# One-region weight layouts and two-tile normalisation at the start of an attention and gMLP block

## The chip, the cores and the metric

The kernel runs on one core of one Trainium2 chip. The core has a matrix engine (TensorE, PE in the profile), a vector engine (VectorE, DVE), a scalar engine (ScalarE, ACT), a general engine (GpSimd, POOL), a queue that issues transfers (SyncE, SP) and 16 DMA engines. Each engine takes its instructions in the order in which the program wrote them, and they meet only at semaphores. PE accumulates into 8 PSUM banks, which DVE and ACT read. The metric is the device time of one execution in microseconds, lower being better, as the median of several runs.

## The reference, cut to what matters

```python
mod = (silu(c) @ w_mod).reshape(1, 6, 1, 448)          # c: (1, 448), w_mod: (448, 2688)
sa, ca, ga, sb, cb, gb = mod[:, 0..5]
h = layernorm(x) * (1 + ca) + sa                        # x: (1, 2048, 448)
qkv = h @ wqkv                                          # wqkv: (448, 1344): q | k | v, 16 heads of 28
x = x + ga * (softmax(q @ k.T * 28**-0.5) @ v) @ wo
h = layernorm(x) * (1 + cb) + sb
z = gelu(h @ w_in); z1, z2 = halves of z (896 each); z2 = layernorm(z2)
x = x + gb * ((z1 * (w_sp @ z2 + b_sp)) @ w_out)        # w_sp: (2048, 2048)
```

All of it is in float32. The change touches only the first three lines and the product with `wqkv`. The other lines take most of the time.

## The kernel before, in words

The kernel keeps float32 accuracy by splitting operands into a high part, rounded for the fast matmul format, and a low part, the rest. A product then takes three matmuls per pair of blocks. Because 448 = 3 x 128 + 64, a product with a depth of 448 takes the eleven steps of the list `STEPS`. Each step `(a, b)` multiplies slot `a` of the one operand by slot `b` of the other. Slots 0, 1, 2 are high parts, 3, 4, 5 the low parts of the same blocks, 6 and 7 hold the last 64 rows, high and low. `STEPS_MAIN` needs slots 0 to 5, and `STEPS_Z` are the two steps on slot 6 of the first operand.

**The rows.** The 2048 rows of `x` are handled in four groups `g` of four tiles `t` of 128 rows. For each group: DVE takes mean and variance of each tile (`ln_stat`, two instructions a tile); POOL turns the variances into 1/sqrt (`ln_rs`, which calls `rstd_of`, two instructions, an addition and a power); DVE normalises (`ln_norm`, L257) and ACT copies 64 columns so that the last block is doubled (L265); PE transposes (L117, sixteen 128x128 pieces in four banks, `c` = 0 to 3); ACT applies scale and shift (L124) and rounds to the high part (L131); DVE subtracts to get the low part (`sub`, L84). The result is `hT[g]`, and its slots come in the order c = 0, 2, 1, 3. `ln_next(g)` does the last three steps for group `g` and, between them, the statistics of group `g + 1`; the power and the normalisation of group `g + 1` come after all four statistics.

**The weights.** `w_mod` is loaded in three pairs of 896 columns, each as four blocks `k` of 112 rows (`load_mod`, L168). The first pair gives `sa` and `ca`: `mod_acc` multiplies the blocks by silu(c) and adds them on DVE (L224, L226), `mod_last` adds the last block in small pieces (L355), PE sums over the partitions. Until `ca` and `sa` are there, no `hT` can be made. `wqkv` is loaded in three parts of columns, each in four row blocks: `v` (columns 896 to 1343), `a` (0 to 511) and `b` (512 to 895), by `load_w`. The last row block has 64 rows and is loaded twice (`load_z`, L87 and L88). Part `v` becomes `wv`; `qk_part` (in it `weight_part`, L95 on ACT for the high part and L84 on DVE for the low part) turns a row block `i` of `a` and `b` into `wqk`. The row blocks come in the order 0, 2, 1, 3.

**The order.** There is no planner here: each engine does what the text of the program lists, in that order. After the first group's `hT[0]` PE computes V of the first four tiles (`v_mm`, L273, 44 matmuls), then `qk_unit((0, 3), 0)`, two blocks of q and k at a time over the eleven steps (L288, 22 matmuls), then the transposes of group 1 (in `ln_next(1)`), the blocks 1 and 2 (22 matmuls, L288), the V of tiles 4 and 5 (22 matmuls, L273), the transposes of group 2, and so on. `qk_unit` ends with ACT writing the high part from PSUM (L298) and DVE the low part (L84, `ql`), after which the two banks are free, and SP stores both to scratch memory. Seven PSUM banks go round in one ring, in the order of `bank(...)` calls. Short matmuls on idle data (`pe_fill`, L215) fill gaps of PE in the first 18 us.

**SP** issues all these transfers in one queue, with eight semaphores in turn, so a transfer's issue waits until the eighth before it has landed, and for its buffer.

Later stages (the attention, the output projection, the gMLP) are not touched.

Of the kernel before, what the change touches and what calls it, by code (L numbers as in the profile page):

```python
# [8 lines left out]
F32 = mybir.dt.float32  # L9
# [7 lines left out]
S, D, H, DH, FH = 2048, 448, 16, 28, 896  # L17
# [11 lines left out]
STEPS = STEPS_MAIN + STEPS_Z  # L29
# [1 line left out]


@with_exitstack
def tile_adaln_mha_gmlp(ctx, tc, x, wqkv, wo, w_in, w_spT, b_sp, w_out, cT, w_mod, out):
# [48 lines left out]
    def sub(eng, dst, a, hi):  # L83
        eng.tensor_tensor(out=dst, in0=a, in1=hi.bitcast(F32), op=ALU.subtract)  # L84

    def load_z(eng, dst, src):
        eng.dma_start(dst[0:64], src)  # L87
        eng.dma_start(dst[64:128], src)  # L88

    def weight_part(dst, i, raw, hi_eng, lo_eng, zero=True, c0=0):  # L90

        cs = slice(c0, c0 + raw.shape[-1])
        h = dst[:, i if i < 3 else 6, cs]
        if hi_eng is act:
            act.activation(h, raw, AF.Copy)  # L95
        else:
            hi_eng.tensor_copy(h, raw)
        if i < 3:
            sub(lo_eng, dst[:, 3 + i, cs], raw, h)
        else:  # L100
            sub(lo_eng, dst[0:64, 7, cs], raw[0:64], h[0:64])
            if zero:
                pool.memset(dst[64:128, 7, cs].bitcast(F32), 0.0)

    def rstd_of(var, rs, n):

        pool.tensor_scalar(out=rs, in0=var, scalar1=EPS, scalar2=None, op0=ALU.add)
        pool.tensor_tensor(out=rs, in0=rs, in1=mhalf[:, :n], op=ALU.pow)

    def ln_transpose(xns, full_pool, dsts, scol, bcol, engs, los=(pool,) * 4, mid=None, after=None):  # L110

        tps = []
        for c in range(4):
            tp = bank("tp")
            tps.append(tp)
            for t in range(4):
                pe.transpose(tp[:, t * 128 : (t + 1) * 128], xns[t][:, c * 128 : (c + 1) * 128], ident)  # L117
        if mid:
            mid()
        for c in (0, 2, 1, 3):  # L120
            tp = tps[c]
            f = full_pool.tile([128, 512], F32, name="hfull")
            if engs[c] is act:
                act.activation(f, tp, AF.Identity, scale=scol[:, c : c + 1], bias=bcol[:, c : c + 1])  # L124
            else:
                engs[c].tensor_scalar(
                    out=f, in0=tp, scalar1=scol[:, c : c + 1], scalar2=bcol[:, c : c + 1], op0=ALU.mult, op1=ALU.add
                )
            hi = dsts[:, c if c < 3 else 6, :]
            if engs[c] is act:  # L130
                act.activation(hi, f, AF.Copy)  # L131
            else:
                engs[c].tensor_copy(hi, f)
            if c < 3:
                sub(los[c], dsts[:, 3 + c, :], f, hi)
            else:
                sub(los[c], hi[64:128], f[64:128], hi[64:128])
            if after:
                after(c)
# [16 lines left out]
    e1 = early.enter_context(tc.tile_pool(name="e1", bufs=2))  # L156
# [3 lines left out]
    wms, xts, raws = {}, {}, {}  # L160

    def bank(name):
        return ring.tile([128, 512], F32, name=name, tag="s")

    def load_mod(pair, eng):
        for k in range(4):
            wms[pair, k] = e1.tile([112, 2, D], F32, name="wm", tag=("wm", "wm", "raw")[pair], bufs=4)
            eng.dma_start(wms[pair, k], w_mod[:, pair, k])  # L168

    def load_x(g, eng):  # L170
        xg = e1.tile([128, 4, D], F32, name="xg")
# [3 lines left out]
            xts[4 * g + t] = xg[:, t, :]  # L175


    PARTS = {"v": (2 * D, D, "raw"), "a": (0, 512, "wm"), "b": (512, 384, "raw")}

    def load_w(kind, i, eng):  # L180
        c0, n, tag = PARTS[kind]
        raw = e1.tile([128, 2 * D], F32, name="raw", tag=tag, bufs=4)[:, :n]
        if i < 3:
            eng.dma_start(raw, wqkv[i * 128 : (i + 1) * 128, c0 : c0 + n])
        else:
            load_z(eng, raw, wqkv[384:448, c0 : c0 + n])
# [54 lines left out]
    def ln_stat(g, ts):  # L241
        if g not in mv1:
            mv1[g] = e1.tile([128, 4, 2], F32, name="mv"), e1.tile([128, 4], F32, name="rs")
        for t in ts:
            st = e1.tile([128, 6], F32, name="st", bufs=4)
            dve.bn_stats(out=st, in_=xts[4 * g + t])
            dve.bn_aggr(out=mv1[g][0][:, t, :], in_=st)

    def ln_rs(g, a, e):
        mv, rs = mv1[g]  # L250
        rstd_of(mv[:, a:e, 1], rs[:, a:e], e - a)

    def ln_norm(g, ts):
        mv, rs = mv1[g]
        for t in ts:
            xn = e1.tile([128, 512], F32, name="xn", bufs=4)
            dve.tensor_scalar(  # L257
                out=xn[:, :D],
                in0=xts.pop(4 * g + t),
                scalar1=mv[:, t, 0:1],  # L260
                scalar2=rs[:, t : t + 1],
                op0=ALU.subtract,
                op1=ALU.mult,
            )
            act.activation(xn[:, D:], xn[:, 384:D], AF.Copy)  # L265
            xn1.setdefault(g, []).append(xn)

    def v_mm(kts, steps=STEPS, own=None):
        pvs = [ps_o.tile([128, 512], F32, name="pv", tag="o") if kt == own else bank("pv") for kt in kts]
        for j, (a, b) in enumerate(steps):  # L270
            for kt, pv in zip(kts, pvs):
                g, t = divmod(kt, 4)
                pe.matmul(pv[:, :D], hT[g][:, a, t * 128 : (t + 1) * 128], wv[:, b, :], start=j == 0, stop=j == NST - 1)  # L273
        return list(zip(kts, pvs))

    def v_copy(kt, pv):
        act.activation(V[:, kt, :, 0:DH], pv[:, :D].rearrange("p (h d) -> p h d", d=DH), AF.Copy)
# [1 line left out]
    def v_tile(kt):  # L279
        v_copy(*v_mm((kt,))[0])  # L280

    def qk_unit(ms, g, mid=None):
        pqs = [bank("pq") for _ in ms]
        for j, (a, b) in enumerate(STEPS):
            if mid and j in mid:
                mid[j]()
            for m, pq in zip(ms, pqs):
                pe.matmul(pq, wqk[:, b, m * 128 : (m + 1) * 128], hT[g][:, a, :], start=j == 0, stop=j == NST - 1)  # L288
        for m, pq in zip(ms, pqs):
            hi = stage.tile([128, 512], F32R, name="qh")  # L290
            lo = stage2.tile([128, 512], F32R, name="ql")
            if mid:
                f = stage.tile([128, 512], F32, name="qf")
                act.activation(f, pq, AF.Copy)
                act.activation(hi, f, AF.Copy)
                sub(pool, lo, f, hi)
            else:
                act.activation(hi, pq, AF.Copy)  # L298
# [90 lines left out]
    for i in (0, 2, 1, 3):  # L389
        load_w("a", i, sp)  # L390
# [32 lines left out]
    for i in (0, 2, 1, 3):  # L423
        load_w("b", i, sp)
    pvs = v_mm((0, 1, 3, 2), [STEPS[j] for j in (0, 1, 2, 3, 6, 4, 5, 7, 8, 9, 10)], 3)
    ln_stat(1, (0, 1))
    qk_part("a", 0, dve)
    qk_part("a", 2, dve)
    ln_stat(1, (2, 3))
    ln_rs(1, 0, 4)  # L430
    qk_part("a", 1, dve)
    qk_part("a", 3, dve)
    load_mod(1, sp)
    for a in pvs:
        v_copy(*a)
    ln_norm(1, range(4))
    qk_unit((0, 3), 0)

    def ln_next(g):

        if g + 1 < NG:
            ln_transpose(
                xn1.pop(g), e1, hT[g], cols["ca"], cols["sa"], (act,) * 4, (dve,) * 4, None,
                lambda c: ln_stat(g + 1, ((0, 2, 1, 3).index(c),)),
            )
            ln_rs(g + 1, 0, 4)
            ln_norm(g + 1, range(4))
        else:
            ln_transpose(xn1.pop(g), e1, hT[g], cols["ca"], cols["sa"], (act,) * 4, (dve,) * 4)

    ln_next(1)
    load_x(3, sp)
    qk_unit((1,), 0)
    qk_unit((2,), 0)
    for i in (0, 2, 1, 3):
        qk_part("b", i, dve)
    load_mod(2, sp)
    for g in range(1, NG):
        if g == 3:
# [32 lines left out]
        if g + 1 < NG:  # L492
            ln_next(g + 1)
# [831 lines left out]
```

## Time and profile before

| | us |
|---|---|
| median of 3 runs | 1411.46 (1411.13 to 1413.48) |
| the profiled execution's own time | 1415.13 |
| its span, from the first to the last instruction | 1413.3 |
| PE busy | 1399.0 (99%) |
| DVE busy | 1011.3 (72%) |
| ACT busy | 787.5 (56%) |
| POOL busy | 284.9 (20%) |

Times are counted from the first instruction of the profiled execution. A row of the timeline gives start, time, engine, line, operation, the names written and read, the shapes and the count; in brackets stands how long the engine had been idle and what ended that. Rows that follow each other on one engine start a little before the row ahead of them has ended, since instructions are pipelined; a distance between two starts is what an instruction costs in a stream. A row of the chain gives start, length and what. A row of the waits gives who waited for whom, the total, the number of times and the longest. A row of the windows gives a stretch, its length, the busy time of each engine with the number of instructions in parentheses, the granted PE clock, the busy share of the 16 DMA engines and the GB/s that they moved.

### The profile page before, as it was taken

What the parts mean: (1) busy time and instruction counts of PE and PEld (TensorE: products, weight loads), DVE (VectorE), ACT (ScalarE), POOL (GpSimd) and SP (SyncE); (2) the same over time, 40 slices, a digit from 0 to 9 for tenths busy, and PEclk for the clock granted to TensorE, in tenths of its full rate; (3) what the DMA queues carried; (4) which work ended last, traced back from release to release, by engine and by line L of the source; (5) the groups of instructions that cost most, each with busy time, mean ns of one, the idle gap of its engine ahead of it and who ended that gap; (6) DMA issues with size and microseconds to landing.
All of it is one profiled execution on the core that took longest, in us unless ns stands there. A gap on an engine that the chain in (4) does not pass through costs nothing.

```text
span 1413.3 us, 20323 instructions
## 1 busy us (share of the span) xinstructions
PE 1399.0 (99%) x7180; PEld 985.4 (70%) x7180; DVE 1011.3 (72%) x1700; ACT 787.5 (56%) x1532; POOL 284.9 (20%) x276
## 2 busy tenths in 40 slices
PE   8999999999999999999999999999999999999998
PEld 7888655555555555555555555988998888887888
DVE  7778888888888888888888850751366655677474
ACT  3723677777777777777677779363243543434211
POOL 3033312212314243313200021000142430001000
PEclk9999999999999999999999999999999999999999
DMA  9564635555455556654423001434103333444453
GB/s 247 162 177 154 189 104 175 166 160 152 157 166 160 159 164 179 175 154 154 120 68 75 21 18 58 172 122 138 45 15 105 105 112 112 151 139 136 136 176 112
DMA packets 98252, 186.99 MB, mean 132 GB/s; under 512 B 16614, under 2 KB 28006, under 8 KB 95606
## 3 DMA queue, kind: packets, MB, share of 16 engines
q1 hardware_dynamic: 95722, 181.87, 42.5%
q10 hardware_dynamic: 2430, 3.84, 0.7%
q8 instruction: 56, 0.92, 0.3%
q14 instruction: 44, 0.36, 0.1%
HBM read 130.42 MB, written 50.45 MB: 128 GB/s over the span
## 4 chain that ended last, share of the span: by engine, by line
PE 95%; DVE 2%; DMA 2%; ACT 1%; issue 0%; POOL 0%; SPq 0%; ACTq 0%; DVEq 0%
PE st_ps L559 19%; PE o_ps L574 17%; PE mt L528 17%; PE acc L1099 6%; PE acc L1098 6%; PE acc L1100 6%; PE z_ps L1024 5%; PE z_ps L910 5%; PE pq L288 4%; PE wo_ps L780 3%; PE pv L273 2%; PE y_ps L1205 2%; PE y_ps L1206 2%; PE y_ps L1204 2%; DMA raw_sp<-ws_scr 1%; PE tp L117 1%
## 5 line engine op out<-in xcount | busy, mean ns | idle before, releaser
L533 DVE TENSOR_REDUCE pm<-mt 128x1 f32<-128x512 f32 x1024 | 631.6, 682 | 110.3 <-PE mt L528 110.2
L563 ACT ACTIVATE P<-st_ps 128x512 f32<-128x512 f32 x1024 | 513.2, 622 | 151.6 <-PE st_ps L559 151.2
L559 PE MATMUL st_ps<-qst,kst 128*128 128x512 f32 x1024 | 408.0, 409 | 0.1
L528 PE MATMUL mt<-kst,qst 128*128 128x512 f32 x1024 | 403.0, 394 | 0.0
L559 PEld LDWEIGHTS st_ps<-qst,kst 128*128 128x128 f32 x1024 | 191.0, 187 | 150.2 <-issue 82.2
L574 PE MATMUL o_ps<-P,V 128*32 128x512 f32 x2048 | 247.5, 598 | 0.0
L528 PEld LDWEIGHTS mt<-kst,qst 128*128 128x128 f32 x1024 | 192.5, 188 | 33.0 <-ACT P L563 0.7
L986 ACT ACTIVATE wsp_h<-raw_sp 128x512 fp32r<-128x512 f32 x112 | 70.1, 631 | 172.8 <-PE acc L1100 106.4
L681 POOL TENSOR_TENSOR ws_raw<-ws_raw 128x512 f32<-128x512 f32 x80 | 103.0, 1287 | 280.3 <-DMA ws_raw<-in_w_spT_dram 280.1
L84 DVE TENSOR_TENSOR wsp_l<-raw_sp,wsp_h 128x512 fp32r<-128x512 f32 x112 | 81.1, 735 | 90.7 <-ACT wsp_h L986 89.9
L574 PEld LDWEIGHTS o_ps<-P,V 128*32 128x32 f32 x2048 | 54.1, 109 | 123.9 <-issue 116.7
L1099 PE MATMUL acc<-wsp_l,heapA 128*128 128x512 f32 x224 | 88.2, 394 | 1.8 <-DVE wsp_l L84 1.8
L1098 PE MATMUL acc<-wsp_h,heapA 128*128 128x512 f32 x224 | 88.0, 393 | 1.2 <-ACT wsp_h L986 1.2
L1100 PE MATMUL acc<-wsp_h,heapA 128*128 128x512 f32 x224 | 87.9, 392 | 0.0
L1099 PE MATMUL acc<-wsp_l,heapB 128*128 128x512 f32 x174 | 67.7, 389 | 0.0
L1098 PE MATMUL acc<-wsp_h,heapB 128*128 128x512 f32 x174 | 67.7, 389 | 0.0
L1100 PE MATMUL acc<-wsp_h,heapB 128*128 128x512 f32 x174 | 67.7, 389 | 0.0
L288 PE MATMUL pq<-heapD,heapD 128*128 128x512 f32 x196 | 62.3, 392 | 0.0
L1028 DVE BATCH_NORM_STATS2 stz<-z 128x6 f32<-128x448 f32 x32 | 19.9, 625 | 50.4 <-ACT z L1027 30.1
L1099 PEld LDWEIGHTS acc<-wsp_l,heapA 128*128 128x128 f32 x224 | 42.3, 189 | 11.2 <-DVE wsp_l L84 2.5
L1098 PEld LDWEIGHTS acc<-wsp_h,heapA 128*128 128x128 f32 x224 | 42.5, 190 | 10.7 <-ACT wsp_h L986 1.6
L1100 PEld LDWEIGHTS acc<-wsp_h,heapA 128*128 128x128 f32 x224 | 42.5, 190 | 9.0
(205 smaller groups left out, 1594.8 us busy)
## 6 DMA issues: line engine op xcount, KB each, us to landing
ws_raw<-in_w_spT_dram SPq DMA_DIRECT2D x160, 256.0 KB
ws_scr<-ws_raw SPq DMA_DIRECT2D x80, 256.0 KB
raw_sp<-ws_scr SPq DMA_DIRECT2D x80, 256.0 KB
kst<-qk_scr SPq DMA_DIRECT2D x45, 224.0 KB
qst<-qk_scr SPq DMA_DIRECT2D x45, 224.0 KB
raw_sp<-in_w_spT_dram SPq DMA_DIRECT2D x32, 256.0 KB
qk_scr<-qh SPq DMA_DIRECT2D x28, 256.0 KB
qk_scr<-ql SPq DMA_DIRECT2D x28, 256.0 KB
```

Of the source, the lines that this page charges most:

```text
L84: eng.tensor_tensor(out=dst, in0=a, in1=hi.bitcast(F32), op=ALU.subtract)
L288: pe.matmul(pq, wqk[:, b, m * 128 : (m + 1) * 128], hT[g][:, a, :], start=j == 0, stop=j == NST - 1)
L528: pe.matmul(mt, qst[h % 3][:, t * 128 : (t + 1) * 128], kst[h % 3][:, kb * 512 : (kb + 1) * 512], start=True, stop=True)
L533: dve.tensor_reduce(out=pms[h][:, t, kb : kb + 1], in_=mt, axis=AX.X, op=ALU.max)
L559: pe.matmul(st, kst[h % 3][:, kt * 128 : (kt + 1) * 128], qst[h % 3][:, qb * 512 : (qb + 1) * 512], start=True, stop=True)
L563: act.activation(p, st, AF.Exp, scale=SCALE)
L574: pe.matmul(otile[h][32 * qb : 32 * qb + 32, :], V[:, kt, h, :], ptiles.pop((u, qb)), start=kt == 0, stop=kt == NT - 1)
L681: pool.tensor_tensor(out=a, in0=a, in1=b, op=SUMS[i // 16][2])
L910: pe.matmul(ps_t, w1[:, b, f * 128 : (f + 1) * 128], h2T[g][:, a, :], start=j == 0, stop=j == NST - 1)
L1098: pe.matmul(acc[i], zh, hi, start=st == 0, stop=False)
L1099: pe.matmul(acc[i], zh, lo, start=False, stop=False)
L1100: pe.matmul(acc[i], zl, hi, start=False, stop=st == 7)
```

## The change

Four things change.

1. On the host `w_mod` is stored with pair and block outermost, so that one transfer of 112 x 896 values reads 401,408 consecutive bytes (before, rows of 3,584 bytes 43,008 apart), and `wqkv` is stored as three arrays, `w_v`, `w_a`, `w_b`, so that a row block is consecutive too (before, rows of 1,792, 2,048 or 1,536 bytes 5,376 apart). The sizes and the number of the transfers and their order in the queue stay.
2. For group 1 the statistics of all four tiles come ahead of the first two `qk_part("a", ...)`, the powers are taken for two tiles at a time, and the normalisation of tiles 0 and 1 (with its ACT copies) stands between the second and the third `qk_part("a", ...)`; tiles 2 and 3 stay behind the copies of V.
3. In `ln_next` the power of two tiles follows the second and the fourth statistics, and tiles 0 and 1 are normalised behind the third (that is, ahead of c = 3); tiles 2 and 3 stay at the end.
4. `qk_unit((0, 3), 0)` takes its steps in the order `HI_FIRST`: first the seven with a high weight slot (0, 1, 2, 6), then the four with a low one (3, 4, 5, 7).

```diff
-            eng.dma_start(wms[pair, k], w_mod[:, pair, k])
+            eng.dma_start(wms[pair, k], w_mod[pair, k])
...
-    PARTS = {"v": (2 * D, D, "raw"), "a": (0, 512, "wm"), "b": (512, 384, "raw")}
+    PARTS = {"v": (2 * D, w_v, "raw"), "a": (0, w_a, "wm"), "b": (512, w_b, "raw")}
...
-            eng.dma_start(raw, wqkv[i * 128 : (i + 1) * 128, c0 : c0 + n])
+            eng.dma_start(raw, w[i * 128 : (i + 1) * 128, :])
...
+    HI_FIRST = [p for p in STEPS if p[1] in (0, 1, 2, 6)] + [p for p in STEPS if p[1] in (3, 4, 5, 7)]
...
-        for j, (a, b) in enumerate(STEPS):
+        for j, (a, b) in enumerate(order):
...
     ln_stat(1, (0, 1))
+    ln_rs(1, 0, 2)
+    ln_stat(1, (2, 3))
+    ln_rs(1, 2, 4)
     qk_part("a", 0, dve)
     qk_part("a", 2, dve)
-    ln_stat(1, (2, 3))
-    ln_rs(1, 0, 4)
+    ln_norm(1, (0, 1))
     qk_part("a", 1, dve)
     qk_part("a", 3, dve)
     load_mod(1, sp)
     for a in pvs:
         v_copy(*a)
-    ln_norm(1, range(4))
-    qk_unit((0, 3), 0)
+    ln_norm(1, (2, 3))
+    qk_unit((0, 3), 0, order=HI_FIRST)
+
+    def ln_step(g, t):
+        ln_stat(g, (t,))
+        if t % 2:
+            ln_rs(g, t - 1, t + 1)
+        if t == 2:
+            ln_norm(g, (0, 1))
...
-                lambda c: ln_stat(g + 1, ((0, 2, 1, 3).index(c),)),
+                lambda c: ln_step(g + 1, (0, 2, 1, 3).index(c)),
             )
-            ln_rs(g + 1, 0, 4)
-            ln_norm(g + 1, range(4))
+            ln_norm(g + 1, (2, 3))
...
-        "w_mod": _np.asarray(inputs["w_mod"]).reshape(4, 112, 3, 2, 448).transpose(1, 2, 0, 3, 4),
+        "w_mod": _np.asarray(inputs["w_mod"]).reshape(4, 112, 3, 2, 448).transpose(2, 0, 1, 3, 4),
```

More of the change, by code (lines that the diff above doesn't have):

```diff
@@ L33, in tile_adaln_mha_gmlp @@
 @with_exitstack
-def tile_adaln_mha_gmlp(ctx, tc, x, wqkv, wo, w_in, w_spT, b_sp, w_out, cT, w_mod, out):
+def tile_adaln_mha_gmlp(ctx, tc, x, w_v, w_a, w_b, wo, w_in, w_spT, b_sp, w_out, cT, w_mod, out):
     nc = tc.nc
@@ L175, in load_x @@
             xts[4 * g + t] = xg[:, t, :]
[L178 removed]
+    PARTS = {"v": (2 * D, w_v, "raw"), "a": (0, w_a, "wm"), "b": (512, w_b, "raw")}
     def load_w(kind, i, eng):
[L181 to L182 removed]
+        c0, w, tag = PARTS[kind]
+        raw = e1.tile([128, 2 * D], F32, name="raw", tag=tag, bufs=4)[:, : w.shape[1]]
         if i < 3:
[L184 removed]
+            eng.dma_start(raw, w[i * 128 : (i + 1) * 128, :])
         else:
[L186 removed]
+            load_z(eng, raw, w[384:448, :])
         raws[kind, i] = raw
@@ L280, in v_tile, with qk_unit @@
         v_copy(*v_mm((kt,))[0])
-    def qk_unit(ms, g, mid=None):
+    HI_FIRST = [p for p in STEPS if p[1] in (0, 1, 2, 6)] + [p for p in STEPS if p[1] in (3, 4, 5, 7)]
+    def qk_unit(ms, g, mid=None, order=STEPS):
         pqs = [bank("pq") for _ in ms]
-        for j, (a, b) in enumerate(STEPS):
+        for j, (a, b) in enumerate(order):
             if mid and j in mid:
```

4 lines of the change are left out of this document (3 added, 1 removed).

## The prediction

> **What bounds the kernel now.** The page comes first: PE is busy in all but 14 us of the span. So work of the other engines counts only where PE waits for it.
>
> ```profile
> span 1413.3 us, 20323 instructions
> PE 1399.0 (99%) x7180; PEld 985.4 (70%) x7180; DVE 1011.3 (72%) x1700; ACT 787.5 (56%) x1532; POOL 284.9 (20%) x276
> ```
>
> The chain of work that ended last then says where that is. From 47.13 on it is PE, instruction after instruction. Ahead of that it is a transfer of `w_mod` and then mostly DVE. What moves the start of the last row but three moves the end. The other rows give PE's pace: 1.75 us for sixteen transposes, 9.97 / 44 = 0.227 for a matmul of L288, 8.96 / 44 = 0.204 for one of L273.
>
> ```profile
> 3.06 9.05 DMA wm<-in_w_mod_dram
> ...
> 18.48 8.78 PE pv L273 x41
> ...
> 47.13 0.66 PE tp L117 x4
> ...
> 61.95 1.75 PE tp L117 x16
> ...
> 69.94 9.97 PE pq L288 x44
> ...
> 79.92 8.96 PE pv L273 x44
> ```
>
> The waits of the first 30 us show what the start loses to transfers: 1.0 us of DVE for `wm`, whose layout changes, and 1.0 us for `x`, whose layout doesn't.
>
> ```profile
> DVE acc L226 <- DMA wm<-in_w_mod_dram: 1.0, 1, 1.0
> DVE st L246 <- DMA xg<-in_x_dram: 1.0, 1, 1.0
> ```
>
> **Part 1, the layouts.** The number, size and order of transfers stay; only their speed can change. The windows give the speed of `wm` at the start, of `x` alone (one region), of a pair of `w_mod` alone, and at 1089 and 1091 of two transfers of 256 KB, the first in rows 8 KB apart, the second in one region (the last two columns are the busy share and GB/s).
>
> ```profile
> 5.00:13.00 8.00, 7.18 (x36) 7.02 (x36) 4.66 (x10) 0.51 (x2) 2.37 (x4) 1.00 1.02 249
> 41.00:42.50 1.50, 1.50 (x9) 1.38 (x8) 1.26 (x3) 0.00 (x0) 0.09 (x1) 1.00 0.82 344
> 52.00:58.00 6.00, 6.00 (x29) 5.06 (x28) 4.36 (x11) 2.62 (x5) 1.26 (x2) 1.00 0.94 252
> 1089.50:1090.60 1.10, 1.10 (x6) 0.91 (x6) 0.64 (x1) 0.42 (x1) 0.00 (x0) 1.00 0.67 237
> 1091.50:1093.00 1.50, 1.50 (x9) 1.23 (x8) 0.33 (x1) 0.63 (x1) 0.00 (x0) 1.00 0.66 186
> ```
>
> Strided `w_mod` moves 249 and 252 GB/s with the DMA engines full, one-region `x` 344 with them not even full. But the last two rows speak the other way: 237 / 0.67 = 354 GB/s when busy for strided rows, 186 / 0.66 = 282 for one region. I take the nearer rows, `w_mod` against `x`. At 344 instead of 249 GB/s the four blocks (1.6 MB) take 4.7 us instead of 6.4, so each lands 0.4 to 1.8 us sooner; by the second block, 0.9. That is about the one wait of 1.0 us. The wait for `x`, ahead of it on DVE, stays. DVE's work between there and 25.78 (below) has no other wait for a transfer, so all of it moves forward by 1.0. **Term: -1.0.** Ends: -2.0, if less traffic also lets `x` land sooner, so that both waits go; +0.7, if one region is slower by the last two rows (0.99 against 0.74 us of full DMA for 256 KB, over the 0.8 MB of two blocks).
>
> [...]
>
> **Part 2, group 1 and the low weights last.** Rows of the three engines around the first `qk_unit`:
>
> ```profile
> 25.78 0.63 DVE L246 BATCH_NORM_STATS2 st<-xg 128x6 f32<-128x448 f32 x1
> 27.27 0.67 DVE L84 TENSOR_TENSOR heapD<-raw,heapD 128x512 fp32r<-128x512 f32 x1
> 27.86 0.68 DVE L84 TENSOR_TENSOR heapF<-raw,heapD 128x512 fp32r<-128x512 f32 x1
> 32.15 1.78 DVE L257 TENSOR_SCALAR xn<-xg,mv,rs 128x448 f32<-128x448 f32 x4 [0.94 <-POOL rs L108]
> ...
> 24.32 0.63 ACT L95 ACTIVATE heapD<-raw 128x512 fp32r<-128x512 f32 x1 [0.24 <-DMA raw<-in_wqkv_dram]
> 27.29 1.85 ACT L277 ACTIVATE V<-pv 128x448 f32<-128x448 f32 x4 [1.13 <-PE pv L273]
> 34.02 0.26 ACT L265 ACTIVATE xn<-xn 128x64 f32<-128x64 f32 x1 [0.17 <-DVE xn L257]
> 34.18 1.07 ACT L298 ACTIVATE qh<-pq 128x512 fp32r<-128x512 f32 x2
> ...
> 27.70 1.55 PE L288 MATMUL pq<-heapD,heapD 128*128 128x512 f32 x6
> 32.73 2.89 PE L117 MATMUL tp<-ident,xn 128*128 128x128 f32 x16
> 35.38 0.94 PE L288 MATMUL pq<-heapD,heapD 128*128 128x512 f32 x3
> ```
>
> On the clock of before (the -1.0 moves all of this alike): DVE's statistics of two tiles cost 27.27 - 25.78 = 1.49, a low part 0.59. The new order puts four statistics (2.98) and two low parts (1.18) ahead of the first two normalisations, which run from 29.94 to 30.83 (1.78 / 4 each). POOL has the power long ready by then. ACT copies 64 columns of each tile (0.26), and these copies now stand ahead of its rounding of row blocks 1 and 3. Before, block 1 was rounded at 24.32; now ACT waits for DVE, copies until 31.1, and block 1 is rounded at 31.75, block 3 at 32.3.
>
> PE starts the unit at 27.70. The new step order gives it four steps on row blocks 0 and 2, eight matmuls, until 29.51. The fifth step needs block 1: PE stands until 31.75, that is **2.2 us**. Fourteen matmuls remain (3.17), the low parts are ready in time (DVE subtracts block 3 until about 33.0, PE asks for it at 34.5), and the unit ends at 34.92 instead of 32.73. That low weights come last costs or saves nothing by itself: before, PE took 5.03 us for 22 x 0.227 = 4.99.
>
> The transposes lose a wait: before they took 35.38 - 32.73 = 2.65 for 1.75 of work, now tile 3 is normalised by about 34, so they end at 36.67. PE is 1.3 late there. ACT is late by less: its `qh` starts at 34.92 instead of 34.18, **+0.75**, and its chain of roundings with it. The copies of V come behind the later rounding, from 32.3 to 34.15, still ahead of PE's need for their banks.
>
> **Part 3, `ln_next(1)`.** This part decides, because here ACT and DVE feed PE.
>
> ```profile
> 39.16 0.77 ACT L124 ACTIVATE hfull<-tp,col_sa,col_ca 128x512 f32<-128x512 f32 x1
> 45.77 1.06 ACT L298 ACTIVATE qh<-pq 128x512 fp32r<-128x512 f32 x2
> ...
> 39.31 0.67 DVE L84 TENSOR_TENSOR heapD<-hfull,heapD 128x512 fp32r<-128x512 f32 x1
> 39.89 0.62 DVE L246 BATCH_NORM_STATS2 st<-xg 128x6 f32<-128x448 f32 x1
> 40.76 0.69 DVE L84 TENSOR_TENSOR heapD<-hfull,heapD 64x512 fp32r<-64x512 f32 x1
> 41.48 0.63 DVE L246 BATCH_NORM_STATS2 st<-xg 128x6 f32<-128x448 f32 x1
> 43.80 1.78 DVE L257 TENSOR_SCALAR xn<-xg,mv,rs 128x448 f32<-128x448 f32 x4 [1.47 <-POOL rs L108]
> ...
> 6.18 0.72 POOL L108 TENSOR_TENSOR rs<-rs,mhalf 128x2 f32<-128x2 f32 x1
> 42.73 1.03 POOL L108 TENSOR_TENSOR rs<-rs,mhalf 128x4 f32<-128x4 f32 x1
> ```
>
> With +0.75 the third statistics (39.89) start at 40.64 and take 0.75. Then come the normalisations of tiles 0 and 1 until 42.3 and ACT's copies until 42.55. Only behind them does ACT scale c = 3, at 42.55 instead of 39.16. The low part followed by 1.60 (40.76), so 44.15; the last statistics 0.72 later, 44.87. From there to the normalisation it was 43.80 - 41.48 = 2.32 with a power over four columns of 1.03; over two it takes 0.72, so 2.01, and the normalisation starts at 46.88. From it to `qh` was 45.77 - 43.80 = 1.97 with four tiles; with two, 0.89 less, so `qh` starts at 47.96. That is 2.2 later than 45.77. The last four transposes wait for a bank which that `qh` and its `ql` free (they are the row at 47.13), so PE's endless stretch starts **2.2 us** later. The rest of PE's path is shorter: 22 matmuls from 36.67 to 41.66, V of tile 4 held until 44.85 by the late c = 3, V of tile 5 done by 47.5. **Term of parts 2 and 3: +2.2.** Ends: +1.4, if ACT's 0.75 doesn't arise; +2.7, with half a microsecond for waits between POOL, DVE and ACT that I put at nothing.
>
> **What costs nothing.** `ln_next(2)` and `ln_next(3)` get the same detour, some 1 to 2 us, but between two groups of transposes PE has 44 matmuls (9.5 us); without that cover each would cost what part 3 does. Three more additions and powers run on POOL, with nothing queued behind them. On SP the loads of the second pair of `w_mod` wait for the buffers of part `a`, which are free 2 us later; behind them stand only the stores of the first unit, themselves later, and the third group of `x`, needed only after 50.
>
> **Part 4, the clock.** PE's new gap has a price if the clock is lowered after it. Rows of before show both cases:
>
> ```profile
> 1302.72 0.51 PE L1098 MATMUL acc<-wsp_h,heapA 128*128 128x512 f32 x1 [1.19 <-ACT wsp_h L986]
> 1304.11 0.50 PE L1099 MATMUL acc<-wsp_l,heapA 128*128 128x512 f32 x1 [0.89 <-DVE wsp_l L84]
> 1300.00:1310.00 10.00, 7.92 (x27) 5.82 (x26) 4.26 (x6) 3.24 (x6) 3.50 (x4) 0.83 0.57 175
> ...
> 13.84 1.10 PE L321 MATMUL tp<-ident,xn 128*128 128x128 f32 x8 [1.62 <-DVE xn L257]
> 12.50:15.00 2.50, 1.16 (x11) 1.16 (x12) 2.50 (x4) 0.51 (x2) 0.00 (x0) 1.00 1.05 255
> ```
>
> Two gaps, 1.19 and 0.89 us with one matmul between, were followed by a clock of 0.83 over the ten us, that is 1.7 us lost; a gap of 1.62 was not (clock 1.00). A gap of 2.2 lies just past these. I take 0, and +1.7 as the end. [...]
>
> **The sum.** The profiled span is 1413.3, its own time 1415.13, 3.67 above the median of the runs. -1.0 + 2.2 + 0 = +1.2: a span of 1414.5, and against the median 1411.46 + 1.2 = **1412.7**.
>
> **The rivals.**
> [...]
> *Layouts idle*: strided rows as fast as regions. The rows at 1089 and 1091 speak for it, the row at 52 against. 1411.46 + 2.2 = 1413.7.
> *Whole start*: both waits for transfers go, -2.0: 1411.6.
> *Faster*: the pairs do what they could. DVE's idle time for POOL (0.94 at 32.15, 1.47 at 43.80) leaves the chain, with 1.0 at the start: -3.4, so 1408.0. Its place is ACT's rounding of block 1: it decides if this isn't held by the copies, so that the first unit ends by 32.7 less the gain of the start. The order of ACT's rows speaks against it.
> [...]
>
> **How the numbers follow.** Forecast 33%, clock cut 25%, layouts idle 15%, whole start 12%, faster 9%, regions slower 6%. The forecast's own range, by the ends of its terms without a cut, is 1411 to 1414. The range for 8 in 10 takes in all but the faster case and the worst of the slow ones: 1410.0 to 1415.9. About 0.2% (2.8 us) is what a measurement of this kernel can tell from no change. Over 1414.3 lie regions slower, half of the clock cuts, half of layouts idle (with a cut on top) and a rest of the forecast, 32%; under 1408.6 the faster case and a rest of the whole start, 10%; 58% lie between.
>
> **What would show it.** Right: the wait of DVE for `wm` gone and the first L273 matmul at 17.5; DMA over 300 GB/s between 5 and 13; in the first L288 stretch a gap of PE near 2 us, ended by ACT's L95; ACT's L265 rows ahead of the third L95; PE without gaps from 48 to 49 on. Wrong: PE through the first unit without a gap; an end of the start phase that moves by over 2 us; a clock under 1.00 between 30 and 40.

## The result and the profile after

The changed kernel takes 1415.28 us (median of 12 runs, 1413.38 to 1419.90), the kernel before in the same series 1411.81 (12 runs, 1410.40 to 1414.46). The ratio is 1.0026, with a 95% interval of 1.0017 to 1.0036: slower by about 3.5 us, where the forecast was 1.2 slower. The profiled execution of after took 1415.45 with a span of 1413.7.

The page of after (span; busy time of each engine) looks like the one of before: PE still fills 99% of a span that is 0.4 us longer, and POOL has six instructions more.

```profile
span 1413.7 us, 20328 instructions
PE 1397.3 (99%) x7180; PEld 984.1 (70%) x7180; DVE 1010.8 (72%) x1700; ACT 787.2 (56%) x1532; POOL 287.2 (20%) x282
```

So the two profiled spans alone would say "no change". Two rows of PE's timeline, the last group of `pc` matmuls, which ends the modulation of group 0, and the first `mt` of the attention, say where the difference is. First before (the row at 47.73, V behind the transposes of group 2, is used further down):

```profile
17.86 0.50 PE L361 MATMUL pc<-ones,acc 112*128 112x1 f32 x4
...
47.73 4.75 PE L273 MATMUL pv<-wv,heapD 128*128 128x448 f32 x22
...
90.67 0.39 PE L528 MATMUL mt<-kst,qst 128*128 128x512 f32 x1
```

and after:

```profile
17.33 0.51 PE L364 MATMUL pc<-ones,acc 112*128 112x1 f32 x4
...
94.91 0.39 PE L539 MATMUL mt<-kst,qst 128*128 128x512 f32 x1
```

The modulation ends 0.53 us earlier, and from there to the first `mt` it is 77.58 instead of 72.81 us, **4.77 more**; together +4.24. Behind that the order of the work is the same in both. The rest took longer in the profiled execution of before: its tail has the two gaps and the lowered clock that the prediction quoted at 1302, after's tail had one gap of 0.99 at 1300. That hides 3.4 us of the 4.2 in the spans. I call the distance between the two rows the **start distance**, and compare kernels by it, because it hardly depends on the execution as long as the clock isn't cut inside it: three kernels whose order is that of before gave 72.81, 72.83 and 72.84.

The chain of waits of after (start, duration, what) shows the same from another side. PE carries the end without interruption only from 67.12 on, 20 us later than before.

```profile
3.06 8.52 DMA wm<-in_w_mod_dram
11.68 1.15 DVE acc L226
...
30.56 0.62 ACT heapD L95
31.23 4.85 PE pq L291 x13
...
44.04 0.68 ACT hfull L124
...
64.17 0.52 DVE xn L257
...
65.83 0.50 ACT qh L301
66.38 0.69 DVE ql L84
67.12 0.66 PE tp L117 x4
```

The waits of the first 30 us (us in total, times, longest) still have DVE waiting for `wm`, 0.9 instead of 1.0, and for `x`, 0.7:

```profile
DVE acc L226 <- DMA wm<-in_w_mod_dram: 0.9, 1, 0.9
DVE st L246 <- DMA xg<-in_x_dram: 0.7, 2, 0.5
```

The places themselves stand in the timelines of after (in brackets the idle time ahead of a row, and what ended it): PE in the first unit, at V of tile 4, and at the transposes of group 3; then ACT.

```profile
27.16 2.01 PE L291 MATMUL pq<-heapD,heapD 128*128 128x512 f32 x8
31.23 1.26 PE L291 MATMUL pq<-heapD,heapD 128*128 128x512 f32 x4 [2.06 <-ACT heapD L95]
36.14 1.91 PE L117 MATMUL tp<-ident,xn 128*128 128x128 f32 x16
46.15 2.92 PE L273 MATMUL pv<-wv,heapD 128*128 128x448 f32 x13 [1.27 <-DVE heapD L84]
67.12 0.66 PE L117 MATMUL tp<-ident,xn 128*128 128x128 f32 x4 [0.37 <-DVE ql L84]
...
29.97 0.26 ACT L265 ACTIVATE xn<-xn 128x64 f32<-128x64 f32 x1 [6.74 <-DVE xn L257]
30.40 0.26 ACT L265 ACTIVATE xn<-xn 128x64 f32<-128x64 f32 x1 [0.17 <-DVE xn L257]
30.56 0.61 ACT L95 ACTIVATE heapD<-raw 128x512 fp32r<-128x512 f32 x1
43.78 0.26 ACT L265 ACTIVATE xn<-xn 128x64 f32<-128x64 f32 x1 [0.17 <-DVE xn L257]
43.95 0.76 ACT L124 ACTIVATE hfull<-tp,col_sa,col_ca 128x512 f32<-128x512 f32 x1
```

PE does eight matmuls of the first unit, stands for 2.06 us, and is released by ACT's rounding of row block 1 (L95), which stands behind the two copies (L265). At 46.15 it stands again, 1.27 us, for the low part of c = 3, whose scaling (L124, 43.95) stands behind two more copies. At 67.12 it stands 0.37 us, in a place that the prediction had put at nothing.

The windows of after (the last three columns are the granted clock, the share of the DMA engines and GB/s) add two things: 278 GB/s for `wm`, not 344, and half the clock for at least 3.3 us, from 1 us behind the end of the gap on.

```profile
5.00:13.00 8.00, 5.78 (x36) 5.59 (x36) 5.25 (x12) 0.51 (x2) 2.38 (x4) 1.00 1.01 278
32.30:35.60 3.30, 3.30 (x9) 2.62 (x8) 1.04 (x3) 1.41 (x5) 0.00 (x0) 0.50 0.87 248
36.00:40.00 4.00, 4.00 (x28) 3.53 (x27) 2.70 (x6) 3.83 (x7) 0.00 (x0) 1.00 0.65 202
```

### The profile page after: what moved, and what is told of

It is laid out like the page before. It is cut to its first block, busy times and chain, and to the rows that moved or that the text cites. A ratio compares the mean times of both kernels' runs of the same rounds, so it can differ in the third digit from the quotient of the medians.

```text
span 1413.7 us, 20328 instructions
## 1 busy us (share of the span) xinstructions
PE 1397.3 (99%) x7180; PEld 984.1 (70%) x7180; DVE 1010.8 (72%) x1700; ACT 787.2 (56%) x1532; POOL 287.2 (20%) x282
## 4 chain that ended last, share of the span: by engine, by line
PE 93%; DVE 2%; DMA 2%; ACT 1%; issue 0%; POOL 0%; SPq 0%; ACTq 0%; DVEq 0%; POOLq 0%
PE st_ps L570 19%; PE o_ps L585 17%; PE mt L539 17%; PE acc L1110 6%; PE acc L1111 6%; PE acc L1109 6%; PE z_ps L1035 5%; PE z_ps L921 5%; PE pq L291 4%; PE wo_ps L791 3%; PE y_ps L1216 2%; PE y_ps L1217 2%; PE y_ps L1215 2%; PE pv L273 1%; DMA raw_sp<-ws_scr 1%; DMA wm<-in_w_mod_dram 1%
```

## The experiments

The theory was that of the prediction: two holds, one in group 1 and one in `ln_next`, both made of ACT's copies standing ahead of work that PE needs. The rivals were the cut of the clock, and layouts that do nothing. The start distances of all runs (start of the last `pc` group to the first `mt`, us, each from one profiled execution), with the ratios of the medians to before in the same series:

| Run | What it is | Start distance | against before | Ratio, 95% interval |
|---|---|---|---|---|
| before | | 72.81 | | |
| after | | 77.58 | +4.77 | 1.0026 (1.0017 to 1.0036) |
| e1 | before + layouts | 72.83 | +0.02 | 0.9992 (0.9981 to 1.0002) |
| e2 | after without layouts | 77.60 | +4.79 | 1.0022 (1.0008 to 1.0035) |
| e3 | after + idle matmuls ahead of the gap | 76.03 | +3.22 | 1.0026 (1.0014 to 1.0039) |
| e4 | after, first unit in the old step order | 75.34 | +2.53 | 1.0014 (1.0001 to 1.0027) |
| e5 | before + group 1 and low weights last | 73.69 | +0.88 | 1.0017 (1.0006 to 1.0029) |
| e6 | before + new `ln_next` | 75.10 | +2.29 | 1.0009 (0.9997 to 1.0022) |
| e7 | after, group 1's copies behind the roundings | 74.06 | +1.25 | 1.0010 (0.9996 to 1.0024) |
| e8 | pairs of powers, all norms behind | 72.82 | +0.01 | 0.9991 (0.9979 to 1.0002) |
| e9 | e8 + ten idle matmuls | 70.89 | -1.92 | 0.9982 (0.9973 to 0.9991) |
| e10 | e1 with `w_mod` of 128 partitions | 72.84 | +0.03 | 0.9994 (0.9985 to 1.0004) |
| e11 | e9 with `w_mod` of 128 partitions | 70.91 | -1.90 | 0.9987 (0.9978 to 0.9997) |
| e12 | e9, first unit in the old step order | 71.79 | -1.02 | 0.9988 (0.9979 to 0.9997) |

### The layouts alone, and everything but the layouts

e1 is before with the two layouts; e2 is after with the old ones.

```diff
-            eng.dma_start(wms[pair, k], w_mod[:, pair, k])
+            eng.dma_start(wms[pair, k], w_mod[pair, k])
```

> The kernel before with the layouts alone. Theory (layouts bring 0.5 us, the order costs all the rest): DVE's first piece of mod_last starts 0.4 to 0.6 us earlier than at 15.30, nothing later is touched, PE's endless stretch starts 0.3 to 0.6 us earlier than 47.13, and the median is 0 to 0.7 us under that of before. Rival (the layouts themselves cost, for instance because whole regions load slower later): 1 us or more over before.

> The changed kernel with the old layouts: parts 2 to 4 alone. Theory: the gap of PE in the first unit (2.1 us) and what follows are there as in the changed kernel, only 0.5 us later, so before + 3 to + 4.5 us. Rival (the layouts cost): within 1 us of before.

The start distance doesn't depend on the layouts (+0.02, and 77.60 against 77.58), and the median of e1 isn't over that of before, while e2 has nearly the whole of after's loss (1413.96 against 1410.60). So the loss is in the order. The windows of e1 show what the layouts do to the transfers:

```profile
5.00:13.00 8.00, 7.02 (x36) 6.83 (x36) 5.41 (x13) 0.51 (x2) 2.25 (x4) 1.00 1.02 264
```

264 GB/s, with the 16 engines as full as before (1.02 in both). With the old layout it was 249 (before), 252 (e2), 261 (e5) and 263 (e6), with the new one 278 (after), 264 (e1), 254 (e3), 263 (e4) and 270 (e7): the means differ by 10 GB/s, and the two ranges overlap. The last `pc` group began at 17.86, 17.62, 17.10 and 16.97 in four profiles with the old layout (before, e2, e5, e6; mean 17.39) and at 17.33, 17.12, 17.44, 17.07 and 16.59 in five with the new one (after, e1, e3, e4, e7; mean 17.11). So the gain is about 0.3 us, less than the spread between executions, and the profiled execution of before had the latest start of these nine. Neither this nor the ratio of e1 can tell it from nothing.

### Group 1 alone, and `ln_next` alone

e5 gives before only the new order of group 1 with `HI_FIRST`; e6 gives it only the new `ln_next` (the powers of group 1 stay as in before, one over four columns, other than the expectation below says).

> The kernel before with part 2 alone (group 1 and the step order; old layouts, old ln_next). Theory (two separate holds of ACT, one in group 1, one in ln_next): the gap of PE of 2.1 us in the first unit is there, ACT's qh of that unit is late by 0.8 us without a half clock and by 2.2 with one, and the first mt matmul comes that much later than 90.67: 91.4 without, 92.9 with. Rival (ln_next alone carries the loss): the first mt matmul within 0.3 us of 90.67.

> The kernel before with part 3 alone (the new ln_next; old layouts, old group 1 but for its powers). Theory: no gap in the first unit; ACT scales c = 3 some 2.6 us later than at 39.16, PE has a gap of about 0.5 us ahead of the last two steps of tile 4's V, the last four transposes of group 2 wait 1.4 us longer, and the later groups another 0.5; first mt matmul 92.0 to 92.7. Rival (group 1 alone carries the loss): within 0.3 us of 90.67.

PE's timeline of e5:

```profile
30.99 1.20 PE L291 MATMUL pq<-heapD,heapD 128*128 128x512 f32 x4 [2.05 <-ACT heapD L95]
...
34.30 1.91 PE L117 MATMUL tp<-ident,xn 128*128 128x128 f32 x16
35.97 0.94 PE L291 MATMUL pq<-heapD,heapD 128*128 128x512 f32 x3
```

and of e6:

```profile
43.34 2.92 PE L273 MATMUL pv<-wv,heapD 128*128 128x448 f32 x13 [1.77 <-DVE heapD L84]
...
48.39 4.74 PE L273 MATMUL pv<-wv,heapD 128*128 128x448 f32 x22
...
64.32 0.66 PE L117 MATMUL tp<-ident,xn 128*128 128x128 f32 x4 [0.38 <-DVE ql L84]
64.73 2.48 PE L273 MATMUL pv<-wv,heapD 128*128 128x448 f32 x11
```

In e5 the gap of 2.05 is there, without a cut of the clock (1.0). The unit takes 7.37 us, 26.93 to 34.30 (the prediction had 7.22), PE is 1.35 late behind the transposes (35.97 - 17.10 = 18.87 us behind the last `pc` group, where before needs 35.38 - 17.86 = 17.52), and 0.88 of it is left at the first `mt`. In e6 the first unit is that of before, V of tile 4 is held for 1.77, and PE reaches the V behind the transposes of group 2 at 48.39, which is 31.42 us behind its last `pc` group (16.97) where before needs 47.73 - 17.86 = 29.87, so 1.55 more; then the transposes of group 3 wait 0.38 for `ql` and take 2.26 instead of 1.66, and PE ends 2.29 late. So the holds add: 0.88 + 2.29 = 3.17. After has 4.77. What is missing is 1.6.

The expectations gave times of the first `mt`, which also move with the start. That of e5, 90.79, would even fit the rival, but its last `pc` group was 0.76 earlier than in before; by the start distance it is the theory's 0.8. That of e6, 92.07, lies in the theory's range only because its start was 0.89 early, and the wait at V of tile 4 was expected at 0.5, not 1.77. The medians give the two edits the other way round, +0.17% for e5 and +0.09% for e6. Their intervals overlap, and the profiled execution of e5 was the second fastest of its ten, with a granted clock of 1.0 over the whole execution where eight of the others had 0.996 to 0.999. So the median of e5 may hold cuts of the clock that its profile doesn't have; that isn't shown.

### Filling the gap

e3 is after with nine idle matmuls ahead of the first unit. They write a bank that the unit overwrites, so only their time is added.

```diff
+        for _ in range(fill):
+            pe.matmul(pqs[0], wqk[:, 0, 0:128], hT[g][:, 0, :], start=True, stop=True)
-    qk_unit((0, 3), 0, order=HI_FIRST)
+    qk_unit((0, 3), 0, order=HI_FIRST, fill=9)
```

> The changed kernel with nine idle matmuls of 128x512 ahead of the first unit, written into its first bank before the real ones start: PE has no gap, the real matmuls still can't end before row block 1 is rounded. Theory (the gap lowers the clock): the unit ends 1.2 to 1.6 us earlier than at 36.1, no half clock near 32, median 1 to 1.5 us under the changed kernel. Rival (the clock plays no part): the unit ends at the same time, median as the changed kernel.

PE's timeline of e3:

```profile
29.34 3.20 PE L293 MATMUL pq<-heapD,heapD 128*128 128x512 f32 x12
...
34.66 1.91 PE L117 MATMUL tp<-ident,xn 128*128 128x128 f32 x16
```

With PE busy through the wait the clock stays full (1.0 over the whole profiled execution), the transposes behind the unit start at 34.66 instead of 36.14, and the start distance falls by 1.55 to 76.03, which is the sum of e5 and e6 within 0.05. So the cut of the clock cost 1.55 us in the profiled execution of after. The median doesn't show it: 1414.37, with the same ratio as after. Its interval is as wide as the effect, and a profile tells nothing of the other executions, where the same gap may or may not be followed by a cut (in e5 it wasn't). What the cut costs in the median stays open.

### The old step order in the changed kernel

```diff
-    qk_unit((0, 3), 0, order=HI_FIRST)
+    qk_unit((0, 3), 0)
```

> The changed kernel with the old order of steps in the first unit. Theory (low weights last makes it worse, since more matmuls are left behind the late row block 1): twelve instead of eight matmuls come ahead of it and ten instead of fourteen behind it, so the unit ends at least 0.9 us earlier; PE's wait is in two pieces (about 0.9 for the first low part, 1.2 for row block 1), so a half clock is less likely; median 1 to 2.2 us under the changed kernel. Rival (low weights last helps): median at or over the changed kernel.

```profile
28.65 0.73 PE L291 MATMUL pq<-heapD,heapD 128*128 128x512 f32 x2 [0.68 <-DVE heapD L84]
...
33.66 1.91 PE L117 MATMUL tp<-ident,xn 128*128 128x128 f32 x16
```

The old order asks for a low part after four matmuls. PE waits 0.68 for DVE to make it, and then has enough to do until block 1 is rounded; the second wait that was expected didn't come. The rows of the unit show no half clock (two matmuls that stand together take 0.63 to 0.73 us, in after 1.05 at a granted clock of 0.50), and the start distance is 2.24 shorter; 1.55 of that is the clock, by e3, so the order itself is worth 0.69. The prediction's sentence that low weights last costs nothing is wrong in this kernel.

### ACT's copies behind its roundings

e7 leaves DVE's order as it is in after and moves ACT's copies of tiles 0 and 1 behind the roundings of blocks 1 and 3.

```diff
-    ln_norm(1, (0, 1))
+    ln_norm(1, (0, 1), False)
     qk_part("a", 1, dve)
     qk_part("a", 3, dve)
+    ln_pad(1, (0, 1))
```

> The changed kernel with one move: ACT's copies of the 64 columns of tiles 0 and 1 of group 1 come behind its roundings of row blocks 1 and 3 instead of ahead of them. DVE's order stays. Theory (these two copies hold the rounding): no gap of PE in the first unit, no half clock, the unit ends about 32 instead of 36.1; the loss of ln_next stays, so the first mt matmul at 91.4 to 92.2 instead of 94.9. Rival (the unit waits for DVE's low parts or for banks): the gap stays over 1 us.

PE's timeline of e7:

```profile
26.42 2.90 PE L297 MATMUL pq<-heapD,heapD 128*128 128x512 f32 x12
...
31.43 1.91 PE L117 MATMUL tp<-ident,xn 128*128 128x128 f32 x16
```

The gap is gone: no idle time of PE over 0.1 us in the unit, which ends 5.01 us after it began. Nothing but the two copies of 0.26 us changed place, so it is they, by waiting for DVE in ACT's queue, that held the rounding. The transposes behind the unit then take 1.66 instead of before's 2.65, since the norms are in time, and the start distance is 1.04 shorter than that of e6, which has the same `ln_next`: 74.06 against 75.10. So the new order of group 1 (statistics first, powers in pairs, norms earlier) does gain 1.0 once no rounding stands behind the copies; which of the three brings it wasn't tested. What is left over before, 1.25, is `ln_next`'s 2.29 less this.

### The pairs without the detour

e8 keeps the layouts, the four statistics first, the powers in pairs and `HI_FIRST`, and puts every norm behind the four `qk_part("a", ...)` and, in `ln_next`, behind c = 3.

```diff
     qk_part("a", 0, dve)
     qk_part("a", 2, dve)
-    ln_norm(1, (0, 1))
     qk_part("a", 1, dve)
     qk_part("a", 3, dve)
...
-    ln_norm(1, (2, 3))
+    ln_norm(1, range(4))
...
-        if t == 2:
-            ln_norm(g, (0, 1))
...
-            ln_norm(g + 1, (2, 3))
+            ln_norm(g + 1, range(4))
```

> The changed kernel with the normalisations behind everything that ACT has to do: layouts, four statistics first and powers of two tiles at a time as in the changed kernel, but group 1's four normalisations behind all four qk_part, and in ln_next all four behind c = 3. Theory (the powers in pairs are worth DVE's waits for POOL, 0.9 and 1.3 us, once nothing of ACT is held): no gaps over 0.5 us between 18 and 45, the first mt matmul at 87.6 to 88.5, median 2 to 3 us under before. Rival (the pairs bring nothing, the gain is only that of the layouts): first mt matmul at 89.7 to 90.2, median under before by at most 1.2.

From the second transposes of group 0 on, PE has no gap any more until 1294. Yet the start distance is no better than before's. PE's timeline of e8, and then its windows, say why:

```profile
12.80 1.09 PE L324 MATMUL tp<-ident,xn 128*128 128x128 f32 x8 [2.75 <-DVE xn L257]
```

```profile
14.00:17.50 3.50, 3.50 (x20) 3.50 (x19) 2.87 (x13) 1.93 (x3) 0.00 (x0) 0.52 1.05 303
17.50:24.40 6.90, 6.90 (x25) 6.38 (x25) 4.81 (x11) 3.50 (x6) 2.50 (x3) 0.50 1.02 339
24.40:30.00 5.60, 5.60 (x29) 5.17 (x28) 5.41 (x10) 1.81 (x4) 2.40 (x3) 1.00 0.34 109
```

Ahead of the transposes at 12.80 PE stood for 2.75 us, and half the clock followed for 10.24 us, until 24.4. But a gap at this place needn't have that price. In before it was 1.62 us long, in e4 2.16, in e6 2.34, and in after and e2 these are the rows:

```profile
13.31 1.09 PE L324 MATMUL tp<-ident,xn 128*128 128x128 f32 x8 [2.53 <-DVE xn L257]
...
13.58 1.09 PE L324 MATMUL tp<-ident,xn 128*128 128x128 f32 x8 [2.75 <-DVE xn L257]
```

No half clock followed in these five, in e2 after a gap exactly as long as that of e8: the granted clock was 1.00 from the transposes to 31 in before and after and 1.0 over the whole execution in e6, and from the last `pc` group to the first unit it took 9.8 us in all five, where e8 took 30.83 - 18.92 = 11.91. So the length alone doesn't decide, and what does is open. The profiled execution of e8 is also the slowest of its twelve (1415.48, median 1410.59), with a granted clock of 0.995 over the whole execution where the other eleven have 0.999 or 1.0. By itself 10.24 us at half clock takes 5.12 / 1414 = 0.0036 off that mean (an estimate from these numbers), so no other execution of e8 had a cut of this length, and the median of e8 is hardly explained by it.

### The gap at 10 us filled

```diff
     tp_first(1)
-    pe_fill(5, x3)
+    pe_fill(15, x3)
     tp_first(2)
```

> The order of the run with both pairs of norms behind all four roundings, with ten more of the idle matmuls (L215, 128x128 f32, 0.26 us each where that run shows five in 1.28 us) between the transposes of x tiles 1 and 2, where that run's TensorE stood for 2.75 us and had half its clock for 10.24 us afterwards. Theory A (once TensorE has no gap from the first transposes on, it alone sets the end of the start, and what the gap cost was the clock): no gap over 0.6 us and no half clock before 1290, first pv matmul near 17.4, first mt matmul at 87.0 to 87.5 (before's 90.67, that run's 91.74), median ratio 0.997 to 0.998, so 3 to 4 us less than before. Rival B (what the start gains is given back later, as the 4.2 us of after's start against the 3.5 us between the medians hint, or is lost in the tail's gaps near 1300): first mt near 87, but a ratio of 0.999 to 1.0. Rival C (the clock is cut at random in that stretch, not because of the gap): half clock again between 10 and 40 without a gap ahead of it, first mt at 89 to 92.

Windows of e9, then its PE timeline:

```profile
13.00:40.00 27.00, 26.85 (x149) 23.79 (x148) 24.71 (x57) 16.19 (x31) 7.83 (x10) 1.00 0.91 267
```

```profile
16.43 0.51 PE L364 MATMUL pc<-ones,acc 112*128 112x1 f32 x4
...
87.32 0.39 PE L536 MATMUL mt<-kst,qst 128*128 128x512 f32 x1
```

The clock is full from 13 to 40, PE has no gap over 0.15 us up to 1291, and the first `mt` comes at 87.32, 3.35 earlier than in before and 4.42 earlier than in the profile of e8. That is theory A, but for the first `pv` matmul, which came at 16.80 and not near 17.4. The ratio is 0.9982 (0.9973 to 0.9991), 1408.54 against 1410.88, so 2.3 us. Of the 3.35 only 1.92 is start distance; the other 1.43 lies ahead of it, where the profile of before is the latest of all but e8's. Whether anything is given back later the interval doesn't tell. This version is faster than both kernels.

### `w_mod` over 128 partitions

e10 is e1 with `w_mod` and `c` padded with zeros on the host, so that each block of `w_mod` fills 128 partitions instead of 112; e11 puts the same into e9, with eleven idle matmuls instead of fifteen.

```diff
-            wms[pair, k] = e1.tile([112, 2, D], F32, name="wm", tag=("wm", "wm", "raw")[pair], bufs=4)
+            wms[pair, k] = e1.tile([128, 2, D], F32, name="wm", tag=("wm", "wm", "raw")[pair], bufs=4)
...
-        "w_mod": _np.asarray(inputs["w_mod"]).reshape(4, 112, 3, 2, 448).transpose(2, 0, 1, 3, 4),
+        "w_mod": _np.pad(_np.asarray(inputs["w_mod"]), ((0, 64), (0, 0))).reshape(4, 128, 3, 2, 448).transpose(2, 0, 1, 3, 4),
```

> The layouts alone, with w_mod and c padded with zeros from 448 to 512 rows, so that each of the four transfers of a pair fills 128 partitions instead of 112 (14% more bytes). The tables of both earlier layouts moved 249 to 278 GB/s between 5 and 13 us. Theory A (the 112 partitions are what makes w_mod slow, whatever its layout): 300 GB/s or more between 5 and 13 us, wm no longer waited for, mod_last of c=0 from 14.0 or earlier. Rival B (the bytes alone set it: x, w_v and w_mod share 16 busy engines): the rate stays at 250 to 280, the last wm lands 0.5 to 1 us later than with 112 partitions, first pv matmul 0.3 to 0.9 us later, and the median rises by as much.

> The order without gaps of the run with ten more idle matmuls (first mt matmul 87.32, no gap of TensorE from 4.5 to 1291, ratio 0.9982) with w_mod padded to 128 partitions (the run of that alone: 351 GB/s between 5 and 13, first pv matmul 16.10) and eleven idle matmuls in the place of its fifteen, since the second pair of x tiles is then normalised 0.7 us earlier. Theory A (the two gains lie one behind the other, the transfers ahead of the first pv matmul and the order behind it): first pv matmul at 16.0 to 16.4, first mt 70.5 us behind it at 86.5 to 86.9, ratio 0.9972 to 0.9980, so 0.5 to 1 us less than with the order alone. Rival B (with the earlier start the norms or the copies of group 1 are late again, since x and wqkv don't come earlier): a gap of TensorE of 0.5 us or more between 16 and 90, first mt at 87.2 or later, ratio as with the order alone.

Windows of e10, then of e11:

```profile
5.00:13.00 8.00, 7.09 (x48) 6.91 (x48) 6.42 (x13) 1.03 (x4) 2.25 (x4) 1.00 0.99 351
```

```profile
5.00:13.00 8.00, 8.00 (x54) 8.00 (x54) 5.87 (x13) 1.03 (x4) 2.25 (x4) 1.00 1.01 361
```

With 14% more bytes (the zeros count) the transfers move 351 and 361 GB/s where all kernels with 112 partitions moved 249 to 278, and in e10 the last `pc` group begins at 15.73, earlier than in any of the profiles above. So it was mostly the 112 partitions, and at most a little the rows in place of regions, that made `w_mod` slow; 128 partitions with the old layout weren't run. The 16 DMA engines were as busy both times, 0.98 to 1.03 with 112 and 0.99 and 1.01 with 128, but the rate isn't the same. Why 112 rows take longer is open.

The median of e10 is no clear gain (0.9994, interval across 1), and e11 (0.9987) isn't better than e9. In e11's profile DVE waited 0.72 us for `x` and took the statistics of the second pair at 8.35, where e10 had them at 7.77; the second transposes came at 12.40 instead of 11.71, and the last `pc` group at 16.30, hardly ahead of e9's 16.43. With `wm` early, `x` is what comes last. The start distance, 70.91, is that of e9: neither of the two expectations, since no new gap arose, but the start didn't gain either.

### The old step order where nothing is late

e12 is e9 with the edit of e4.

> The run with ten more idle matmuls, with the first q and k unit in the old order of its products (the low weights of each row block in their old places). Theory A (in the kernel as changed, low weights last cost 2.5 us in the first mt matmul only because row block 1 came late there; with every norm behind the roundings neither order waits): no gap over 0.3 us in the first unit, first mt within 0.3 us of 87.3, median ratio 0.997 to 0.999. Rival B (the roundings of the row blocks come so late that one order still waits, as the unit begins 9.5 us behind the first pv matmul): a gap of 0.3 to 1 us in the first unit, ended by VectorE's or ScalarE's rounding, and first mt 0.3 to 1 us later, so that low weights last is worth something in that order.

```profile
28.91 0.73 PE L291 MATMUL pq<-heapD,heapD 128*128 128x512 f32 x2 [0.67 <-DVE heapD L84]
```

Rival B: a gap of 0.67, ended by DVE's low part, and a start distance 0.90 longer. With the norms behind the roundings, low weights last is worth nearly a microsecond: the low parts are what comes last there. In after it is block 1's rounding, and there the same order costs 0.69, and 1.55 more by the clock in the profiled execution. The ratios of e9 and e12, taken in two series, don't tell the two apart.

## Why the prediction was right or wrong

The side and the main mechanism were right: slower, by two holds of ACT's queue, and 1415.28 lies in the range, near its upper end. The sum was not: +1.2 fell short of the +3.5 between the medians and of the +4.24 at the first `mt`, and its errors didn't cancel: each of the terms made the change look cheaper than it was measured. Of the three signs that the prediction named for being wrong two came, an end of the start that moved by over 2 us and a clock under 1.00 between 30 and 40. By its steps:

- **Part 1, -1.0.** Wrong in its reason, mis-sized by more than half. I took the rate of `x` as that of one region and the rate of `w_mod` as that of strided rows. The two differ also in partitions, 128 against 112, and e10 shows that this is what counts (351 GB/s between 5 and 13, e1 264). The layouts gave about -0.3, not clear of the spread (-0.53 between the two profiles). "Wait gone" failed too: 0.9 us of DVE's wait for `wm` is left.
- **Part 2.** The gap was predicted at 2.2 and is 2.06, ended by L95 behind L265 as written; e5's unit takes 7.37 for 7.22; PE is 1.35 late behind the transposes for 1.3; the delay carried on was +0.75 and is 0.88. Right.
- **"That low weights come last costs or saves nothing by itself".** Wrong: e4 shows that the new order turns a gap of 0.68 into one of 2.06. Before had no gap in the unit, and so couldn't show what the order does once a block is late.
- **Part 3, +2.2 with parts 2 and 3 together,** so 1.45 for `ln_next(1)` alone. e6 measured 1.55 there, and the two together (0.88 + 1.55) are 2.43. Right.
- **"What costs nothing".** Wrong for `ln_next(2)`: it is the rest of e6's 2.29, about 0.7, of which 0.6 at the transposes of group 3. (`ln_next(3)` has no next group, so no detour.) The 44 matmuls cover DVE's detour, but not that the second pair's norms delay ACT's copies, `qh` and DVE's `ql`, which frees a bank for the last four transposes.
- **Part 4, the clock, 0.** Wrong in the profiled execution, by 1.55: a clock cut, to which the prediction gave 25%, came. No row of before decided between 0 and the end of +1.7, since both cases stand there. The upper end of the range, 1415.9, is 1411.46 + 2.2 + 0.7 + 1.5, and the 1.5 for a cut was the author's estimate: no run shows it. What the runs showed in its place is the 1.55 between after and e3. That a cut would come couldn't be told from the length of the gap: of the gaps of 2.05 to 2.09 at this place two were followed by a cut (after, e2) and one wasn't (e5). Nor were two gaps with one matmul between always followed by a cut, as those of 1.19 and 0.89 at 1302 in before were: in e6 gaps of 0.96 and 1.17 there kept the full clock (1.0 over its whole execution).

Together: -0.53 + (0.88 + 2.29 + 1.55) = +4.19, against +4.24 measured at the first `mt`. The medians' +3.5 lies between the parts without the cut (-0.3 + 0.88 + 2.29 = +2.9) and with it (+4.4). The rival "faster" named what decided it, that ACT's rounding isn't held by the copies, and priced it at 1408.0, 3.4 us less; e9, which takes the copies from ahead of the roundings, moves the norms in `ln_next` too and fills one more gap, took 1408.54, but against 1410.88 in its series, so 2.3 less. That the two absolute times are so near is partly chance.

## What to carry to other kernels

An instruction that waits is priced by what stands behind it in its engine's queue: two copies of 0.26 us on an engine that is busy for 56% of the span cost PE 2 us, because they waited for DVE ahead of a rounding. Put early work ahead of nothing that the bound engine needs, then ask what the next late thing is; the best order of the steps depends on it. And compare transfers that differ in one thing only before a rate is credited to a layout.

## What the runs showed of the hardware

- Between 5 and 1290 us the fourteen profiles hold eight gaps of PE of over 2 us. Three were followed by half clock (granted 0.50): 2.06 in after and 2.09 in e2 by 3.4 us of it, 2.75 in e8 by 10.2. Five weren't: 2.05 in e5, 2.16 in e4, 2.34 in e6, 2.53 in after and 2.75 in e2. No shorter gap there (at most 1.77) was followed by a cut, and no cut came without a gap of over 2 us ahead of it. So a long gap is a risk, not a price; idle matmuls took it away in e3 and e9.
- Between 5 and 13 us, where `w_mod` loads, the DMA engines moved 249 to 278 GB/s with `w_mod` on 112 partitions and 351 and 361 with it on 128, busy at 0.98 to 1.03 and at 0.99 and 1.01.
- Apart from the start, executions of the same work differ by more than this change is worth: from the first `mt` to the first matmul of the tail's `acc` group it took 970.6 to 972.8 us over the profiles of all these kernels, from there to the end of PE's last matmul 342.9 to 347.5, neither in step with the edits. So the start distance, which repeats within 0.03 where the order and the cuts of the clock are the same, settled what the medians couldn't.
